# Batch 0 of a local-attention plus token-mixing MoE kernel as one hand-ordered pipeline

## The chip, the cores and the metric

The kernel runs on one core of a Trainium2 chip. The metric is the device time of one execution in microseconds, and the number to forecast is the median of several runs of the changed kernel. Engine names are those of the profile: PE is TensorE (matmuls), PEld its weight loads, DVE is VectorE, ACT is ScalarE, POOL is GpSimd, SP is SyncE, and SPq is the part of SP that issues DMAs.

## The reference, cut to what matters

Eight batches, eight heads, 576 tokens, head size 64. Heads 0 to 3 attend to the last 32 tokens (plain); heads 4 to 7 attend to 32 tokens at a distance of 4 (dilated). The attention output, 576 rows of 512, goes through a token-mixing low-rank product and a two-layer MLP.

```python
rel = pos[:, None] - pos[None, :]
mask_plain = (rel >= 0) & (rel < window)                     # window 32
mask_dil = (rel >= 0) & (rel < window * dilation) & (rel % dilation == 0)
scores = scale * np.matmul(q, k.transpose(0, 1, 3, 2))       # masked with -1e9
scores = scores - np.max(scores, axis=-1, keepdims=True)
attn = np.exp(scores)
attn = attn / (np.sum(attn, axis=-1, keepdims=True) + 1e-09)
x = np.matmul(attn, v)            # heads side by side: (8, 576, 512)
h = x.transpose(0, 2, 1) @ U @ V  # U 576x32, V 32x576
u = x + h.transpose(0, 2, 1)
out = u + np.maximum(u @ w_ch1, 0.0) @ w_ch2   # 512 -> 2048 -> 512
```

## The kernel before, in words

**Groups.** The tokens of a half (plain or dilated, the dilated ones sorted by residue so that its window is local too) are cut into nine tiles of 64 queries with 96 keys each. Two neighbouring tiles make a group of four units, so a batch has nine groups and the kernel 72. In batch 0 and 1 a unit is one tile and two heads: the queries of the two heads stand block-diagonally in a 128x128 operand, and one fp32 matmul (`s`, L380) gives 128 rows by 96 keys. From batch 2 on (`two`, L369) a unit is one head and 128 queries, and its operands are split into a high and a low fp32r part by ACT (L344) and POOL (L345, L348).

**Steps of a group.** `score` does the `s` matmuls. `soften` does mask and row minimum on DVE (L400, with L397 ahead of it from batch 2 on) and the exponential on ACT (L404), which also accumulates the row sums. `turn` transposes p: in batches 0 and 1 on PE (`ptp`, L417) with a DVE copy to SBUF (L421), later on DVE (L430, L433). `weighted` does four `pv` matmuls (L441), the reciprocal of the sums (L442, L443), and four DVE multiplications into `x` for plain tiles or `xp` for dilated ones (L469); the dilated rows then go to their place in `x` by small DMAs (L473).

**Token mixing.** When a batch is complete, `split` makes a high and a low part of x (ACT L487, DVE or POOL L489), `t_mm` multiplies by U (`t`, L509), `t_evict` copies the result in parts, `mix` multiplies by V (`m`, L533) and DVE adds to x (L535).

**MLP.** 12 chunks of 384 tokens. `transp` turns x (L564, later by DVE and DMA) and splits it into `uth`, `utl` (L569, L570). For each of 16 slices f of the hidden layer, `layer1` does 12 matmuls into `ph` (L733), ACT makes `hh` (L738), DVE `hl` (L739), and `layer2` adds nine matmuls to `acc` (L750). The attention and mixing of later batches are put between the matmuls by a table of due positions (`queue`, `slot`).

**Weights.** U, V, w1 and w2 come as float64 in pieces. `weight_step` moves four pieces on by one stage each: `fetch64` (DMA, SP, L194, L196), `narrow_a` (two ACT passes, L203, L204), `narrow_b` (DVE shift L208 and add L210) and the finish, for w1 and w2 `narrow_c` (cast on ACT L214 or DVE L216, remainder on POOL L217). Slice f needs pieces 3+2f and 4+2f.

**Order.** Before, the whole kernel is written in a program order from which a scheduler with priorities decides each engine's stream. Batch 0's operands are loaded by SP; all DMAs of the kernel are issued by SP. The program has eight DMA semaphores which it uses in rotation, so a DMA is issued only when the one eight places earlier has landed. Batch 0 stands wholly ahead of the first chunk; batch 1 is woven into chunk 0.

## Time and profile before

| what | value |
|---|---|
| runs (3) | 1029.8, 1030.41, 1031.37 us; median 1030.41 |
| the profiled execution | 1034.31 us, span of its instructions 1032.5 us, mean granted clock 0.974 |
| PE busy | 994.2 us, 96% of the span |
| PEld, DVE, ACT, POOL busy | 894.7, 645.1, 413.7, 289.5 us |
| chain that ended last | PE 82% |
| first `ph` matmul (start of chunk 0) | 66.39 us |
| first output add of chunk 0, 1, 2, 3 (L775) | 168.23, 263.85, 342.27, 421.12 us |

The profiled execution is 3.9 us above the median; its own time is 1.8 us above its span. A busy share is that of records: matmul ends are modelled, so a PE at 100% is not a PE at its peak. Rows of the timeline give start, duration, engine, line, operation, tiles and the count merged into the row; what stands in brackets at the end is the idle time before it and what ended it.

### The profile page before, as it was taken

How to read it: one execution, taken by the hardware profiler on the slowest of the kernel's cores; microseconds unless marked ns; L12 is line 12 of the kernel's file. 1: busy time of each engine (PE TensorE's matmuls, PEld its weight loads, DVE VectorE, ACT ScalarE, POOL GpSimd, SP SyncE). 2: the span in 40 equal slices, each digit the busy share in tenths (PEclk: the TensorE clock that was granted, in tenths of full speed). 3: DMA queues.
4: the chain of work that ended last, by engine and by line, in shares of the span. 5: the costliest groups of instructions: out<-in, count | busy, mean ns of one | idle time of the engine just before them, and what ended most of it. 6: DMA issues, size and time to landing. Idle time of an engine off the chain costs nothing.

```text
span 1032.5 us, 17337 instructions
## 1 busy us (share of the span) xinstructions
PE 994.2 (96%) x5328; PEld 894.7 (87%) x5328; DVE 645.1 (62%) x2188; ACT 413.7 (40%) x1233; POOL 289.5 (28%) x492
## 2 busy tenths in 40 slices
PE   6589998999999999999999999999999999999998
PEld 6468896998899898998899898999889898999997
DVE  4989768777457863877557873787637874311211
ACT  3867655444234532544333532445424442111110
POOL 0335433243132621434222531325213431000000
PEclk9669898999999999999999999999999999999999
DMA  9658544243232423434232432434223321400000
GB/s 262 206 186 259 182 139 119 76 114 102 64 102 77 123 81 76 120 85 116 74 90 81 124 89 61 129 84 126 85 72 88 115 66 30 126 1 1 31 1 31
DMA packets 96908, 103.03 MB, mean 100 GB/s; under 512 B 12817, under 2 KB 83537, under 8 KB 96817
## 3 DMA queue, kind: packets, MB, share of 16 engines
q1 hardware_dynamic: 96816, 101.94, 34.1%
q8 instruction: 43, 0.70, 0.3%
q14 instruction: 49, 0.39, 0.1%
HBM read 79.86 MB, written 17.30 MB: 94 GB/s over the span
## 4 chain that ended last, share of the span: by engine, by line
PE 82%; DVE 4%; DMA 1%; ACT 1%; issue 1%; POOL 0%; SPq 0%; DVEq 0%; ACTq 0%; POOLq 0%
PE ph L733 36%; PE acc L750 35%; PE pv L441 5%; PE s L369 3%; PE t L509 2%; DVE utl L570 1%; PE s L380 1%; PE m L533 1%; DVE pt L433 1%; DMA raw<-w 1%; DVE pt L430 0%; DMA qkr<-qk 0%; DVE x L469 0%; DVE v L210 0%; DMA x<-xp 0%
## 5 line engine op out<-in xcount | busy, mean ns | idle before, releaser
L750 PE MATMUL acc<-w2h,hh 128*128 128x512 f32 x576 | 228.8, 397 | 0.0
L750 PE MATMUL acc<-w2l,hh 128*128 128x512 f32 x576 | 228.3, 396 | 0.0
L750 PE MATMUL acc<-w2h,hl 128*128 128x512 f32 x576 | 214.0, 397 | 1.7 <-DVE hl L739 1.7
L345 POOL TENSOR_TENSOR qks<-qkr,qks 128x160 fp32r<-128x160 f32 x192 | 104.2, 542 | 379.8 <-ACT qks L344 273.1
L739 DVE SCALAR_TENSOR_TENSOR hl<-ph,hh 128x384 fp32r<-128x384 f32 x192 | 105.9, 552 | 165.2 <-ACT hh L738 164.9
L738 ACT ACTIVATE hh<-ph 128x384 fp32r<-128x384 f32 x192 | 93.3, 486 | 278.0 <-PE ph L733 268.0
L733 PE MATMUL ph<-uth,w1h 128*128 128x384 f32 x768 | 176.3, 343 | 0.1
L404 ACT ACTIVATE p<-p,nmax 128x160 f32<-128x160 f32 (+1 forms) x288 | 116.8, 406 | 148.8 <-DVE nmax L400 140.0
L733 PE MATMUL ph<-uth,w1l 128*128 128x384 f32 x768 | 174.4, 340 | 0.4 <-POOL w1l L217 0.4
L733 PE MATMUL ph<-utl,w1h 128*128 128x384 f32 x768 | 172.3, 338 | 0.0
L733 PEld LDWEIGHTS ph<-uth,w1h 128*128 128x128 f32 x768 | 139.7, 191 | 15.7 <-ACT uth L569 0.7
L733 PEld LDWEIGHTS ph<-uth,w1l 128*128 128x128 f32 x768 | 136.8, 190 | 1.2 <-POOL w1l L217 0.7
L733 PEld LDWEIGHTS ph<-utl,w1h 128*128 128x128 f32 x768 | 135.2, 188 | 1.4
L750 PEld LDWEIGHTS acc<-w2h,hl 128*128 128x128 f32 x576 | 107.7, 189 | 24.8 <-DVE hl L739 2.9
L430 DVE STREAM_TRANSPOSE pt<-p 32x128 f32<-32x128 f32 x384 | 115.9, 302 | 20.8 <-ACT p L404 15.6
L750 PEld LDWEIGHTS acc<-w2h,hh 128*128 128x128 f32 x576 | 108.6, 189 | 15.6
L750 PEld LDWEIGHTS acc<-w2l,hh 128*128 128x128 f32 x576 | 108.6, 189 | 15.0
L344 ACT CAST qks<-qkr 128x288 fp32r<-128x288 f32 x192 | 81.3, 428 | 86.6 <-PE s L369 58.4
L348 POOL TENSOR_TENSOR qks<-qkr,qks 64x128 fp32r<-64x128 f32 x192 | 89.9, 468 | 15.1
L397 DVE TENSOR_TENSOR p<-s,wide_sb 128x160 f32<-128x160 f32 x192 | 60.3, 319 | 48.6 <-PE s L369 46.6
L441 PE MATMUL pv<-v,pt 96*128 96x128 f32 x576 | 81.4, 287 | 7.2 <-DVE pt L421 7.2
L489 POOL TENSOR_TENSOR xhl<-x,xhl 128x256 fp32r<-128x256 f32 (+1 forms) x70 | 50.4, 739 | 130.4 <-ACT xhl L487 69.3
(66 smaller groups left out, 1023.2 us busy)
## 6 DMA issues: line engine op xcount, KB each, us to landing
qkr<-qk SPq DMA_DIRECT2D x192, 144.0 KB, 2.2
raw<-w SPq DMA_DIRECT2D x26, 512.0 KB, 4.6
v<-vv SPq DMA_DIRECT2D x126, 96.0 KB, 2.0
out<-x SPq DMA_DIRECT2D x36, 256.0 KB, 2.2
zd<-z SPq DMA_DIRECT2D x120, 64.0 KB, 2.1
xt<-zd SPq DMA_DIRECT2D x30, 256.0 KB, 2.8
qk<-qk SPq DMA_DIRECT2D x9, 448.0 KB, 9.2
qkr<-qk SPq DMA_DIRECT2D x18, 224.0 KB, 3.9
```

The source lines that it names most:

```text
L344: nc.scalar.copy(out=t[:, 0:QK2], in_=raw)
L345: nc.gpsimd.tensor_tensor(out=t[:, QK2:], in0=raw[:, P:], in1=t[:, P:QK2].bitcast(F32), op=ALU.subtract)
L348: eng.tensor_tensor(out=t[lo, 0:P], in0=raw[lo, 0:P], in1=t[lo, 0:P].bitcast(F32), op=ALU.subtract)
L397: nc.vector.tensor_tensor(out=p_sb[:, u, :], in0=sp[:, 0:KW], in1=wide_sb[:, kind], op=ALU.add)
L404: nc.scalar.activation(out=p_sb[:, u, 0:w], in_=p_sb[:, u, 0:w], func=AF.Exp, bias=nmax[:, u:u + 1], scale=-1.0, accum_out=ssum[:, u:u + 1],)
L430: nc.vector.transpose(out=to[:, :, WIN * (r % 2):WIN * (r % 2 + 1)], in_=p_sb[rs, :, QB * s + WIN * k:QB * s + WIN * (k + 1)])
L441: nc.tensor.matmul(pv[:, u, :], lhsT=pt[:, u, :], rhs=v_sb[:, u % 2, :], start=True, stop=True)
L489: eng.tensor_tensor(out=xl[rs], in0=x[rs], in1=xh[rs].bitcast(F32), op=ALU.subtract)
L733: nc.tensor.matmul(ph, lhsT=w[:, k, :], rhs=u[:, k, :], start=(n == 0), stop=(n == len(seq) - 1))
L738: nc.scalar.activation(out=hh, in_=ph, func=AF.Relu)
L739: nc.vector.scalar_tensor_tensor(out=hl, in0=ph, scalar=0.0, in1=hh.bitcast(F32), op0=ALU.max, op1=ALU.subtract)
L750: nc.tensor.matmul(acc[i], lhsT=h[:, ss], rhs=w, start=(f == 0 and n == 0), stop=(f == FC - 1 and n == 2))
```

## The change

1. **Order.** Batch 0 is written out by hand (`first_batch`), and inside `manual_schedule` the streams of PE, DVE, ACT and SP are exactly as written; POOL's is not. Per turn g: `s` of group g, `ptp` of g-1, `pv` of g-2, softmax of g, the copy of `pt` of g-1, `place` of g-3.
2. **Own DMA ring.** Batch 0's q, k, v and all weight pieces are issued by ACT instead of SP. All 36 loads of batch 0 and the first five pieces (ut, vt and three of w) stand ahead of ACT's first exponential, with ACT's table load behind them.
3. **Compact q.** The zeros of the block-diagonal q are not loaded: two memsets (POOL, DVE) clear `q_sb`, two DMAs per group fill the blocks.
4. **Rows by token, ones beside v, in every batch.** A unit is one head and both tiles of a group. `pv` is eight matmuls with 64 weight columns and 65 moving columns, the two tiles going to partitions 0 to 63 and 64 to 127; the 65th column of v is one, so it yields the row sum and ACT accumulates none. `place` does the reciprocal and one multiplication of 128x256 (two of 64x256 where the two tiles go to different places) instead of four of 64x128.
5. **In batch 0 alone:** the copy of `pt` moves from DVE to ACT; `t` is an fp32 matmul of unsplit x with fp32 U (`t_first`, ten of them), which drops the ten splits; the zero part of `ts` is a memset.
6. **Dilated tiles first** in each batch, and their half of the mixing first.
7. **Part of U and V first.** ut holds the blocks that batch 0 needs (10 instead of 14 columns of 32), vt the middle 384 columns of V; the rest (`uv`) follows behind the first slice of weights. The adds of these pieces and of the first two w pieces move from DVE to POOL.
8. **Weights.** Ahead of the third `uth` ACT's stream has both passes of `narrow_a` for two w pieces (slice 0) and one for two more; before, it had both for seven and one for an eighth. The order of issue inside chunk 0 is the scheduler's in both.

```diff
-TILES = [(0, j) for j in range(NJ)] + [(1, NJ - 1)] + [(1, j) for j in range(NJ - 1)]
+VW = D + 1
+TILES = [(1, j) for j in range(NJ)] + [(0, NJ - 1)] + [(0, j) for j in range(NJ - 1)]
...
-                nc.sync.dma_start(out=r, in_=src[:, h * step:(h + 1) * step])
+                nc.scalar.dma_start(out=r, in_=src[:, h * step:(h + 1) * step])
...
+    def load_q(g):
+        t = early.tile([P, UNITS, KB], F32, tag="k", name=f"k{g}", bufs=NGB)
+        nc.scalar.dma_start(out=t, in_=k0[g])
+        for i in range(2):
+            rs = slice(i * QB, (i + 1) * QB)
+            nc.scalar.dma_start(out=q_sb[rs, g, i], in_=q0[g, rs])
+        loaded[g, 0] = t
...
         nc.scalar.activation(
             out=p_sb[:, u, 0:w], in_=p_sb[:, u, 0:w], func=AF.Exp,
-            bias=nmax[:, u:u + 1], scale=-1.0, accum_out=ssum[:, u:u + 1],
+            bias=nmax[:, u:u + 1], scale=-1.0,
         )
...
+    def product(g, pt):
+        pv = psum.tile([P, UNITS, VW], F32, tag="ps", name=f"pv{g}")
+        for u in range(UNITS):
+            for i in range(2):
+                rs = slice(i * QB, (i + 1) * QB)
+                nc.tensor.matmul(pv[rs, u, :], lhsT=pt[:, u, rs], rhs=loaded[g, 1, i][:, u, :], start=True, stop=True)
+        return pv
...
+        if todo[0][1] is todo[1][1]:
+            todo = [(slice(0, P),) + todo[0][1:]]
+        for rs, x, row, half in todo:
+            n = rs.stop - rs.start
+            dst = x[row:row + n, 0:HALF_D]
+            nc.vector.tensor_tensor(
+                out=dst.rearrange("p (u d) -> p u d", u=UNITS), in0=pv[rs, :, 0:D],
+                in1=ssum[rs].unsqueeze(2).broadcast_to([n, UNITS, D]), op=ALU.mult)
...
+        nc.tensor.matmul(t_ps[0, c], lhsT=u32[rs, u * RANK:(u + 1) * RANK], rhs=x[rs],
+                         start=first, stop=t_count[c] == len(parts))
...
+        for g in range(NGB):
+            for u in range(UNITS):
+                score(g, u)
+            if g >= 1:
+                tp[g - 1] = turn_pe(g - 1, state.pop(g - 1)[0])
+            if g >= 2:
+                pv[g - 2] = product(g - 2, pt.pop(g - 2))
+            for u in range(UNITS):
+                soften(g, u)
+            if g >= 1:
+                copy(g - 1)
+            if g >= 3:
+                place(g - 3, pv.pop(g - 3))
...
+    order = tc.manual_schedule(engines=ORDERED)
+    order.__enter__()
     for g in range(NGB):
-        load_qk(g)
...
+        load_q(g)
         load_v(g, 0)
+        if g in U_AT:
+            pipe[U_AT.index(g)] = fetch64(U_AT.index(g))
+    send(NSMALL + 3)
+    first_batch()
+    order.__exit__(None, None, None)
```

Three places show what stands where. ACT's stream at its start, before (p is the probabilities, nmax the row minimum, ssum the row sum):

```order
L404 ACT_TABLE_LOAD
L404 ACTIVATE p_132,ssum_134<-p_132,nmax_133 128x96 x4
L404 ACTIVATE p_148,ssum_150<-p_148,nmax_149 128x96 x4
L404 ACTIVATE p_186,ssum_188<-p_186,nmax_187 128x96 x4
L404 ACTIVATE p_225,ssum_227<-p_225,nmax_226 128x96 x4
```

The exponentials of group 0 are the second thing ACT does. ACT's stream after, at the end of its issues (k, q, v are batch 0's operands, w the float64 weights):

```order
L305 DMA q_sb<-q 64x256 x2
L313 DMA v_158<-vv 96x520
L179 DMA raw_160<-w 128x4x256
L181 DMA raw_162<-w 128x1024
L179 DMA raw_164<-w 128x4x256
L417 ACT_TABLE_LOAD
L417 ACTIVATE p_166<-p_166,nmax_167 128x96 x4
L417 ACTIVATE p_181<-p_181,nmax_182 128x96 x4
L640 COPY pt_73<-ptp_188 96x512
```

The exponentials now stand behind 41 DMA issues and the table load. PE's stream in batch 0 before, from its first matmul:

```order
L380 MATMUL s_135<-qk_93 128x96 x4
L380 MATMUL s_151<-qk_99 128x96 x4
L417 MATMUL ptp_164<-id_sb,p_132 96x128 x4
L380 MATMUL s_189<-qk_103 128x96 x4
L417 MATMUL ptp_202<-id_sb,p_148 96x128 x3
L441 MATMUL pv_174<-v_97,pt_75 128x128 x4
L417 MATMUL ptp_202<-id_sb,p_148 96x128
```

And after, from its fifth group on:

```order
L451 MATMUL pv_287<-v_118,pt_73 64x65 x8
L394 MATMUL s_319<-k_132,q_sb 128x96 x4
L428 MATMUL ptp_324<-id_sb,p_275 96x128 x4
L451 MATMUL pv_329<-v_124,pt_74 64x65 x8
L394 MATMUL s_363<-k_140,q_sb 128x96 x4
L428 MATMUL ptp_368<-id_sb,p_317 96x128 x4
```

The order of the three steps is fixed, and `pv` is eight matmuls of half the width instead of four. ACT's stream before, from the third `uth` (the last that chunk 0's first matmul needs) to the first `hh`:

```order
L569 CAST uth_624<-tp_649 128x4x128
L204 ACTIVATE raw_619<-raw_619 128x512
L214 CAST w1h_82<-v_644 128x4x128
L203 ACTIVATE v_681<-raw_647 128x512
L204 ACTIVATE raw_647<-raw_647 128x512
L203 ACTIVATE v_690<-raw_669 128x512
L204 ACTIVATE raw_669<-raw_669 128x512
L214 CAST w2h_84<-v_666 128x512
L203 ACTIVATE v_699<-raw_684 128x512
L204 ACTIVATE raw_684<-raw_684 128x512
L738 ACTIVATE hh_0_785<-ph_0_752 128x384
```

After, seven instructions (the cast of w2h, an issue for w, three issues for batch 1's q and k, two casts of us) stand between the third `uth` and these, which end with the first `hh` (us and vs are the parts of U and V that later batches use, v_607 the rest of U and V, the other v and raw are w pieces):

```order
L188 ACTIVATE v_607<-raw_448 128x448
L189 ACTIVATE raw_448<-raw_448 128x448
L188 ACTIVATE v_631<-raw_164 128x512
L188 ACTIVATE v_636<-raw_450 128x512
L181 DMA raw_639<-w 128x1024
L188 ACTIVATE v_725<-raw_595 128x512
L189 ACTIVATE raw_595<-raw_595 128x512
L218 CAST us<-v_607 128x4x32
L212 CAST vs<-v_607 128x64
L212 CAST vs<-v_607 128x256
L179 DMA raw_728<-w 128x4x256
L826 ACTIVATE hh_0_688<-ph_0_656 128x384
```

Between the third `uth` and the first `hh` ACT had nine instructions and now has 18, six of them DMA issues.

More of the change, by code (lines that the diff above doesn't have):

```diff
@@ L59 @@
 H_ON_ACT = 3
-XL_DVE = ((0, 1), (1, 1))
+XL_DVE = ((1, 0),)
 AHEAD = 2
@@ L434, in turn @@
[L434 to L442 removed]
+                o = WIN * k + (QB * (r // 2) if is_wide(g) else 0)
+                nc.vector.transpose(out=pt[WIN * k:WIN * (k + 1), :, rs], in_=p_sb[rs, :, o:o + WIN])
@@ new lines, in turn, with weighted, place @@
+        return pt
+    def weighted(g, pt):
+        place(g, product(g, pt))
+    def product(g, pt):
[5 more added lines that the diff above has]
+        return pv
+    def place(g, pv):
+        b = g // NGB
+        ssum = work.tile([P, UNITS], F32, tag="ssum", name=f"ssum{g}", bufs=2)
+        nc.vector.tensor_scalar(out=ssum, in0=pv[:, :, D], scalar1=1e-9, scalar2=None, op0=ALU.add)
@@ L453, in weighted @@
             else:
-                if xp is None:
+                if i == 0:
                     if b == 0:
-                        xp = early.tile([P, HALF_D], F32, tag="xp", name=f"xp{g}", bufs=XPS)
-                    elif b < SPLIT and g % 2:
-                        xp = spare[:, 0:HALF_D]
-                    else:
-                        xp = work.tile([P, HALF_D], F32, tag="xp", name=f"xp{g}", bufs=1)
-                    part = next(p for p, js in enumerate(DPART) if j in js)
-                row = QB * DPART[part].index(j)
@@ L827, in lay_out @@
+    for a in range(4):
+        blocks[a] = U[a * P:(a + 1) * P]
+        blocks[4 + a] = U[64 + a * P:64 + (a + 1) * P]
+    blocks[8, 0:64] = U[512:576]
+    blocks[8, 64:128] = U[0:64]
+    perm = np.array([token_of(1, s) for s in range(S)])
+    ut = np.zeros((P, NU, RANK), raw)
+    for i, a in enumerate(UB):
+        ut[:, i] = blocks[a]
+    for p in range(NDP):
+        rows = perm[P * p:P * (p + 1)]
+        ut[:len(rows), len(UB) + p] = U[rows]
     vt = np.zeros((4, RANK, P + S), raw)
```

490 lines of the change are left out of this document (259 added, 231 removed).

## The prediction

> **What bounds the kernel now.** I read three views: the busy time by stretch, to see where PE is the bound; then the timeline of the start, because the change is there; then the groups of the first chunk. First the stretches (columns: length, then PE, PEld, DVE, ACT, POOL busy, granted clock, DMA share, GB/s).
>
> ```profile
> 0.00:10.00 10.00, 3.75 (x16) 3.51 (x17) 1.15 (x10) 2.82 (x9) 1.20 (x6) 1.00 0.79 236
> 10.00:20.00 10.00, 7.90 (x56) 7.39 (x56) 7.09 (x45) 4.63 (x24) 0.00 (x0) 0.95 1.05 272
> 20.00:30.00 10.00, 9.00 (x69) 8.52 (x68) 7.56 (x37) 5.47 (x23) 0.00 (x0) 0.88 1.04 319
> ...
> 0.00:66.40 66.40, 42.92 (x221) 35.40 (x221) 48.32 (x179) 36.42 (x120) 13.44 (x17) 0.75 0.73 215
> 66.40:120.90 54.50, 50.40 (x275) 46.46 (x275) 52.06 (x137) 43.11 (x111) 29.66 (x23) 0.90 0.71 227
> 120.90:168.20 47.30, 46.78 (x269) 40.57 (x268) 32.73 (x93) 25.64 (x77) 13.34 (x15) 1.00 0.45 132
> 168.20:178.70 10.50, 6.82 (x25) 4.55 (x24) 9.52 (x27) 4.90 (x16) 3.92 (x8) 0.71 0.53 155
> 178.70:263.90 85.20, 85.15 (x465) 78.11 (x466) 64.31 (x250) 37.73 (x120) 31.15 (x61) 0.98 0.35 97
> 342.30:421.10 78.80, 78.80 (x428) 71.14 (x427) 49.19 (x164) 30.11 (x90) 24.27 (x46) 1.00 0.34 94
> ```
>
> From 178.7 us on PE has no gap, so only fewer or shorter matmuls help there. The change can win in four places: the 66.4 us ahead of chunk 0; its first half, 66.4 to 120.9, where DVE (52.06 of 54.50 us) is the fullest engine; its second half, which PE bounds; and the border of chunks 0 and 1, 168.2 to 178.7. The profiled execution took 1034.31 us against a median of 1030.41; I apply the differences to the median.
>
> **The change part by part.**
>
> *Loads ahead of the first exponential.* Now ACT exponentiates at 6.46 us; after, its stream holds 41 DMA issues first. Timeline rows are start, length, engine, line, operation, tiles, count, and in brackets the idle time ahead and what ended it; SPq issues DMAs.
>
> ```profile
> 0.74 1.28 ACT L404 ACT_TABLE_LOAD   x1 [0.74 <-PEq L847]
> 2.59 0.43 SPq L295 DMA_DIRECT2D qk<-qk  x1
> 6.46 0.37 ACT L404 ACTIVATE p<-p,nmax 128x96 f32<-128x96 f32 x1 [4.44 <-DVE nmax L400]
> 6.74 0.19 ACT L404 ACTIVATION_READ_ACCUMULATOR p<-p,nmax 128x1 f32 x1
> 28.42 0.39 SPq L194 DMA_DIRECT2D raw<-w  x1
> ```
>
> An issue waits for the DMA eight places earlier, so ACT's last one waits until about 4.93 MB (in units of 1000 KB of 1024 bytes; 5.05 million bytes) have landed: eight groups of 515 KB, ut, vt and half a piece of w. The first two rows of stretches moved 2.36 + 2.72 = 5.08 MB in 20 us. Hence 20 us, 0.4 us for the last issue (the 0.39 and 0.43 us rows) and 1.28 us for the table: first exponential at 21.7 us, 15.2 later. Here a rule bears. The Trainium skill, "DMA: Bandwidth & Descriptors", section "Issuing engines are not separate DMA queues", says that DMAs started by different engines share the same 16 DMA engines, and that a second issuer saves only issue time. The share of 1.05 and 1.04 agrees; were it wrong and a second ring brought the 319 GB/s of the third row from the start, 5.05 MB would take 15.8 us and the sum below would be 4.2 us less. The memsets of q and the compact q (4.6 instead of 5.8 MB for q, k and v) lie inside these 20 us, and SP, which issues these loads today, only gets emptier.
>
> *The nine groups.* With operands there, PE sets the pace:
>
> ```profile
> 11.25 0.69 DVE L421 COPY pt<-ptp 96x512 f32<-96x512 f32 x1
> 13.82 1.20 DVE L469 TENSOR_TENSOR x<-pv,ssum 64x128 f32<-64x128 f32 x4 [0.42 <-PE pv L441]
> ...
> 24.99 0.60 PE L417 MATMUL ptp<-id_sb,p 128*96 128x128 f32 x4
> 25.42 1.06 PE L441 MATMUL pv<-v,pt 96*128 96x128 f32 x8
> 26.32 0.28 PE L417 MATMUL ptp<-id_sb,p 128*96 128x128 f32 x1
> 26.43 1.03 PE L380 MATMUL s<-qk 128*128 128x96 f32 x8
> 27.30 0.38 PE L417 MATMUL ptp<-id_sb,p 128*96 128x128 f32 x2
> ...
> 58.36 0.42 DVE L535 TENSOR_TENSOR x<-x,m 128x256 f32<-128x256 f32 x1 [0.78 <-PE m L533]
> ```
>
> From start to start, ptp takes 0.43, pv 0.90, s 0.87 us: 2.2 us a group. ACT needs four exponentials of 0.28 (6.74 less 6.46; the read of the sum falls away) and the copy of 0.69 that it takes from DVE, 1.8; DVE needs less. Eight groups of 2.2 are 17.6 us, the last four exponentials 1.1, the first fp32 `t` 4 x 0.44 = 1.8 (0.44 is twice an s matmul of 0.22; bounds 0.2 and 0.9), a cold stretch of PE 1 to 2: last exponential at about 44 us. The cost of the eight `pv` is put at today's (the last part of this list gives its bounds). `place` with 128x256 lies between the 0.42 us of one add of that size and the 1.20 of four multiplications; I take 0.8.
>
> *The tail to the first `ph`* (timeline).
>
> ```profile
> 57.63 0.47 PE L509 MATMUL t<-xhl,us_d 128*64 128x256 f32 x1 [1.30 <-DVE xhl L489]
> 65.76 0.58 ACT L569 CAST uth<-tp 128x512 fp32r<-128x512 f32 x1
> 66.39 1.65 PE L733 MATMUL ph<-uth,w1h 128*128 128x384 f32 x4
> 66.81 0.62 ACT L214 CAST w1h<-v 128x512 fp32r<-128x512 f32 x1
> 67.31 0.69 ACT L203 ACTIVATE v<-raw 128x512 f32<-128x512 f32 x1
> 68.46 0.67 ACT L203 ACTIVATE v<-raw 128x512 f32<-128x512 f32 x1
> ```
>
> Today's last `t` to the first `ph` is 8.8 us (57.63 to 66.39). Ahead of it come the last group's ptp 0.43, copy 0.69, pv 0.90, place 0.8: 2.8 us. First `ph` at 44 + 11.6, about 55.6 us: **−10.8**. Without the splits it could be 2 earlier; with `t` at 0.9 us, 3 later.
>
> *Chunk 0, first half.* What ACT had narrowed early it narrows now under chunk 0.
>
> ```profile
> 72.17 0.49 ACT L738 ACTIVATE hh<-ph 128x384 fp32r<-128x384 f32 x1 [0.81 <-PE ph L733]
> 120.93 0.49 ACT L738 ACTIVATE hh<-ph 128x384 fp32r<-128x384 f32 x1 [0.29 <-PE ph L733]
> ```
>
> And of the groups of the first 150 us one of POOL (line, engine, tiles, count; busy, mean ns):
>
> ```profile
> L217 POOL TENSOR_TENSOR w1l<-v,w1h 128x512 fp32r<-128x512 f32 x14 | 20.0, 1432 | 29.8 <-ACT w1h L214 15.1 <-DVE w1h L216 11.3 <-DVE ssum L442 3.0
> ```
>
> From the third `uth` to the ninth `hh` ACT's stream holds, before, 19 + 18 passes of `narrow_a`, 15 casts, 24 exponentials and nine `hh`; it took 55.2 us (65.76 to 120.93). After, it holds 48 passes (0.57 each from start to start, 67.31 to 68.46): 27.4 us; 18 casts of 0.50 (66.81 to 67.31): 9.0; 25 issues of 0.4: 10.0; 16 exponentials of 0.28: 4.5; nine `hh` at 0.4 (0.49 less the overlap of the next): 3.6; five small casts of 0.3: 1.5. That is 56 us, and ACT becomes the bound in DVE's place. With 2 to 4 us in which it waits for `ph` or a DMA, 59: **+3.8** (+0.8 with no wait, −3 if PE set the pace at 52). So the ninth `hh` stands at about 114, 7 earlier. POOL takes over the adds of five pieces at up to 1.43 us an instruction; its 29.66 busy of 54.50 us leave room.
>
> *What is left over.* By the ninth `hh` batch 1 is two groups behind today (16 exponentials for 24). Those 4.4 us of PE fall into the second half, where PE has no slack: **+4** (3.5 to 4.4).
>
> *The border.* Today the last rows of batch 1 reach x by a DMA, as the chain of waits shows there (start, length, what):
>
> ```profile
> 162.71 0.58 SPq L473
> 163.34 1.86 DMA x<-spare
> ```
>
> The split of x waits for its landing. The first output add of chunk 0 follows, and it is the start of the border:
>
> ```profile
> 168.23 1.89 DVE L775 TENSOR_TENSOR x<-acc,x 128x512 f32<-128x512 f32 x3 [0.84 <-PE acc L750]
> ```
>
> With dilated tiles first, the plain ones end the batch and no DMA lies ahead of the last mixing. The 10.5 us at the border hold 6.82 of PE at a clock of 0.71, which is 4.8 at full clock: at most 5.7 us can go. I take **−4** (0 to −5.7), since transposes and splits stay.
>
> *`pv` in 63 later groups.* First two groups of weight loads (270 to 660 us), then the timeline around one `pv`:
>
> ```profile
> L441 PEld LDWEIGHTS pv<-v,pt 96*128 96x128 f32 x216 | 27.8, 191 | 0.7
> L509 PEld LDWEIGHTS t<-xhl,us 128*64 128x64 f32 x48 | 6.1, 134 | 1.4 <-issue 0.4
> ```
>
> ```profile
> 324.44 1.05 PE L441 MATMUL pv<-v,pt 96*128 96x128 f32 x8
> 325.25 0.48 PE L750 MATMUL acc<-w2l,hh 128*128 128x512 f32 x1
> ```
>
> Eight records take 0.81 to 0.90 us from start to start, about 110 ns each, of a weight load of 191; so 80 of the 191 ns overlap the next. A load of 64 columns has 134, less 80 is 54 to 57: sixteen such make 0.91 instead of 0.89, 63 times **+1.3**. If loads kept their ratio (134 to 191), 16 x 77 ns is 1.24 and the sum gains +22; if the two halves of the array ran side by side it is −28 (first rival). I take the difference because both rows are of the same unit. The `L750` row starts where the next step follows. The missing sums on ACT and shorter `place` on DVE in later batches cost or win nothing while PE has no gap.
>
> Sum: −10.8 + 3.8 + 4 − 4 + 1.3 = −5.7, from 1030.4 to about **1025**.
>
> **The rivals.** *B, the halves overlap.* Two tiles of 64 columns on different halves could load and multiply at once: pv 0.46 us, −0.45 x 63 = −28, giving about 997. The pv rows speak against it: pace there goes with the load of weights, and one loader is seen busy at a time. The Trainium skill, "TensorEngine Tiling (Array Packing)", section "Key Properties", says that different tiles can execute loads and matmuls in parallel; no row of this trace shows two tiles at work. *C, ACT does not bound chunk 0* (its waits fall into what PE leaves): +3.8 becomes −3 to −6, and the time 1012 to 1018. For it: DVE loses a quarter of its work there. Against: the 56 us. *D, swallowed:* the start is won but the narrowing that moved under chunk 0 gives all of it back, within 0.2% of 1030, about what a measurement of this kernel can tell from no change. For it: the pieces are as many as before, and every one left out ahead is done later. *E, the other side:* ACT's queue blocks. In the first half 25 of its instructions are issues, each standing until a DMA eight places back has landed, with `hh` behind it, for which PE waits.
>
> ```profile
> raw<-w SPq DMA_DIRECT2D x26, 512.0 KB, 4.6
> qk<-qk SPq DMA_DIRECT2D x9, 448.0 KB, 9.2
> ```
>
> The columns are the count, the size of one and the median time from issue to landing. Pieces of 512 KB take 4.6 us to land and under a full queue 448 KB took 9.2. If each of 25 issues stands 0.55 us longer, that is +14, about 1039; it decides from some 8 us of such waits. Against it: the share of 0.71 in that stretch leaves the queue free a quarter of the time.
>
> **How the numbers follow.** The main case, 1019 to 1030, has 0.47, of which 0.05 within 0.2% of today; B 0.12; C 0.13; D 0.13; E 0.15. Faster: 0.42 + 0.12 + 0.13 = 0.67; same: 0.05 + 0.13 = 0.18; slower 0.15. The range takes in the main case, C, D and the nearer half of E: 1006 to 1036 leaves out B and the far half of E.
>
> **What would show it.** The first exponential at 20 to 23 us, pv's 16 records near 0.9 us a group, the first `ph` at 54 to 58, the ninth `hh` at 112 to 117, ACT over 90% busy between these, PE without a gap in the second half, and a border under 7 us. A pv of 0.5 us shows B; an ACT with under 80% busy and the ninth `hh` before 109 shows C; ACT idle ahead of its issues in chunk 0 shows E. The forecast is wrong above all if the price of a 64-column weight load is not the difference I took, or if the weights of the first slices come too late behind ACT's queue.

## The result, and the profile after

The changed kernel takes 1046.33 us (median of four runs, 1046.05 to 1047.01) against 1030.89 for the kernel before: a ratio of 1.0147, 95% interval 1.0128 to 1.0167. It is slower by 15.4 us where 5 to 6 us faster was forecast. The profiled execution took 1047.01 us, 0.7 above its median; the one shown of the kernel before stood 3.9 above its own.

The time by stretch, first as in the prediction and then in three parts: up to the first `ph`, on to chunk 1's first `hh`, the rest (length; PE, PEld, DVE, ACT, POOL busy; granted clock; DMA share; GB/s). Of the kernel after:

```profile
0.00:10.00 10.00, 3.79 (x15) 3.58 (x16) 2.78 (x9) 0.00 (x0) 3.78 (x9) 1.00 0.74 191
10.00:20.00 10.00, 0.55 (x3) 0.30 (x2) 0.80 (x8) 0.00 (x0) 0.00 (x0) 1.00 1.04 253
20.00:30.00 10.00, 3.22 (x14) 2.88 (x15) 0.03 (x1) 3.98 (x10) 0.00 (x0) 1.00 1.02 290
30.00:40.00 10.00, 10.00 (x81) 8.75 (x80) 3.72 (x30) 5.49 (x16) 0.00 (x0) 1.00 0.07 17
...
68.80:125.40 56.60, 46.81 (x262) 40.25 (x263) 52.50 (x105) 46.21 (x95) 36.58 (x29) 0.93 0.83 268
125.40:188.40 63.00, 55.53 (x363) 45.12 (x363) 39.82 (x123) 28.60 (x79) 18.49 (x21) 0.95 0.42 120
188.40:196.50 8.10, 4.72 (x21) 3.47 (x20) 7.52 (x24) 4.76 (x11) 4.31 (x9) 0.76 0.74 224
...
0.00:68.80 68.80, 40.03 (x290) 31.85 (x290) 21.98 (x116) 24.74 (x65) 10.50 (x15) 0.96 0.49 130
68.80:201.10 132.30, 111.66 (x662) 93.44 (x663) 102.41 (x260) 80.75 (x187) 60.82 (x60) 0.92 0.62 191
201.10:1045.10 844.00, 839.20 (x4954) 742.38 (x4953) 468.90 (x1596) 282.09 (x695) 227.31 (x426) 1.00 0.29 80
```

And of the kernel before, the row from 30 to 40 us and the same three parts:

```profile
30.00:40.00 10.00, 6.03 (x26) 4.35 (x27) 9.71 (x40) 9.82 (x38) 1.42 (x2) 0.63 0.72 200
...
0.00:66.40 66.40, 42.92 (x221) 35.40 (x221) 48.32 (x179) 36.42 (x120) 13.44 (x17) 0.75 0.73 215
66.40:184.40 118.00, 109.65 (x589) 97.22 (x589) 97.93 (x272) 75.34 (x210) 48.88 (x49) 0.91 0.58 178
184.40:1032.50 848.10, 841.61 (x4522) 762.03 (x4520) 498.87 (x1738) 301.94 (x905) 227.14 (x426) 1.00 0.28 80
```

The start is not shorter but 2.4 us longer. The middle is 14.3 us longer. The rest is 4.1 shorter. In the first two parts together PE, DVE and ACT have no more work than before: PE 151.7 us against 152.6, DVE 124.4 against 146.3, ACT 105.5 against 111.8. Only POOL, which took over adds, has more, 71.3 against 62.3, and PE hardly waits for it (0.5 us in the middle, 0.4 before). What grew is idle time. In the first part DVE is busy for 22 of 68.8 us where it was for 48 of 66.4. Of these 26 us, 10.6 are its shifts and adds of weights (1.6 us instead of 12.2); the others the change dropped, merged or gave to ACT. From 30 to 40 us the transfers run at 17 GB/s where the kernel before brought weights at 200, and by the first `ph` seven transfers of weights have landed instead of eleven. The conversion left over comes later: DVE's shifts and adds take 53.5 us in the middle instead of 43.3.

The start of the kernel after in the timeline:

```profile
25.05 1.28 ACT L417 ACT_TABLE_LOAD   x1 [25.05 <-DMA q_sb<-q]
26.35 2.23 ACT L417 ACTIVATE p<-p,nmax 128x96 f32<-128x96 f32 x8
33.66 1.06 PE L428 MATMUL ptp<-id_sb,p 128*96 128x128 f32 x4
34.65 1.14 PE L451 MATMUL pv<-v,pt 96*64 96x65 f32 x16
35.71 2.11 PE L394 MATMUL s<-k,q_sb 128*128 128x96 f32 x8
37.65 0.60 PE L428 MATMUL ptp<-id_sb,p 128*96 128x128 f32 x4
38.18 0.69 PE L451 MATMUL pv<-v,pt 96*64 96x65 f32 x16
38.80 2.11 PE L394 MATMUL s<-k,q_sb 128*128 128x96 f32 x8
40.74 0.60 PE L428 MATMUL ptp<-id_sb,p 128*96 128x128 f32 x4
```

The first exponential comes at 26.35 us. From start to start `ptp` takes 0.53 and `pv` 0.62 us, but `s` 1.94 (38.80 to 40.74), where it took 0.87: a group is 3.09 us, not 2.2. Ahead of 37.6 us `ptp` and `pv` run at half that pace (0.99 and 1.06 us), and `s` at the same 1.94. The view's clock column reads 1.00 for both, so this slow pace of a PE that has just begun is not in it.

The tail, with DVE's and ACT's rows:

```profile
62.51 0.58 ACT L589 CAST uth<-tp 128x512 fp32r<-128x512 f32 x1 [1.65 <-PE tp L584]
63.12 0.69 DVE L590 TENSOR_TENSOR utl<-tp,uth 128x512 fp32r<-128x512 f32 x1 [1.37 <-ACT uth L589]
63.73 0.41 DVE L555 TENSOR_TENSOR x<-x,m 128x256 f32<-128x256 f32 x1
64.20 1.11 PE L584 MATMUL tp<-id_sb,x 128*128 128x128 f32 x4 [1.61 <-DVE x L555]
65.35 0.58 ACT L589 CAST uth<-tp 128x512 fp32r<-128x512 f32 x1 [2.26 <-PE tp L584]
68.83 1.65 PE L821 MATMUL ph<-uth,w1h 128*128 128x384 f32 x4 [0.68 <-ACT uth L589]
```

This is a ring: DVE's add of the next tile (L555) stands behind the `utl` of this one, which waits for `uth`, which waits for the transposes, which wait for the add. Three rounds, 2.84 us from one `uth` to the next.

What PE waited for between the first `ph` and chunk 1's first `hh` (total, times, longest; the first rows), after and then before:

```profile
PE acc L838 <- ACT hh L826: 8.8, 6, 2.9
PE tp L584 <- DVE nmax L413: 2.5, 1, 2.5
```

```profile
PE pv L441 <- DVE pt L421: 4.1, 2, 2.8
PE m L533 <- DVE x L535: 2.5, 2, 1.6
```

PE's idle time in this part is 20.6 us (132.30 less 111.66) against 8.4, and 8.8 of the 12.3 more is a wait for `hh`, which does not occur before; 6.3 of it lie ahead of the ninth `hh`. What stands ahead of one such `hh` in ACT's rows:

```profile
74.47 0.47 ACT L826 ACTIVATE hh<-ph 128x384 fp32r<-128x384 f32 x1
...
81.69 0.68 ACT L189 ACTIVATE raw<-raw 128x512 int32<-128x512 uint32 x1 [0.59 <-DMA raw<-w]
83.38 0.62 ACT L199 CAST w1h<-v 128x512 fp32r<-128x512 f32 x1 [0.46 <-DVE v L195]
86.06 0.62 ACT L199 CAST w2h<-v 128x512 fp32r<-128x512 f32 x1 [0.93 <-DVE v L195]
86.59 0.48 ACT L826 ACTIVATE hh<-ph 128x384 fp32r<-128x384 f32 x1
```

Between the first `hh` and the second lie 12.1 us of passes over weights. ACT is idle for 2.8 of them, for transfers and for DVE; the others are its own work, with five issues among it.

### The profile page after: what moved, and what is told of

Its sections match the earlier page's. It is cut to its first block, busy times and chain, and to the rows that moved or that the text cites. A ratio compares the mean times of both kernels' runs of the same rounds, so it can differ in the third digit from the quotient of the medians.

```text
span 1045.1 us, 17970 instructions
## 1 busy us (share of the span) xinstructions
PE 990.9 (95%) x5904; PEld 867.7 (83%) x5904; DVE 593.3 (57%) x1972; ACT 387.6 (37%) x946; POOL 298.6 (29%) x501
## 4 chain that ended last, share of the span: by engine, by line
PE 83%; DVE 3%; DMA 2%; issue 1%; ACT 1%; SPq 0%; ACTq 0%; DVEq 0%
PE acc L838 37%; PE ph L821 36%; PE pv L451 4%; PE s L381 3%; PE t L531 2%; PE m L553 1%; DMA raw<-w 1%; PE s L394 1%; DMA zd<-z 1%; DMA v<-vv 0%; DVE v L195 0%; DVE x L555 0%; DVE z L563 0%; PE ptp L428 0%; ACT v L188 0%
## 5 line engine op out<-in xcount | busy, mean ns | idle before, releaser
L838 PE MATMUL acc<-w2h,hl 128*128 128x512 f32 x576 | 211.3, 399 | 1.1 <-DVE hl L827 1.1
L821 PE MATMUL ph<-utl,w1h 128*128 128x384 f32 x768 | 175.6, 341 | 0.0
L821 PE MATMUL ph<-uth,w1h 128*128 128x384 f32 x768 | 172.7, 343 | 1.6 <-DVE w1h L201 0.7
L821 PE MATMUL ph<-uth,w1l 128*128 128x384 f32 x768 | 171.8, 340 | 0.5 <-POOL w1l L202 0.5
L417 ACT ACTIVATE p<-p,nmax 128x160 f32<-128x160 f32 (+1 forms) x288 | 109.6, 406 | 132.5 <-DVE nmax L413 131.4
L440 DVE STREAM_TRANSPOSE pt<-p 32x128 f32<-32x128 f32 x432 | 130.1, 301 | 18.7 <-ACT p L417 13.3
L838 PEld LDWEIGHTS acc<-w2h,hh 128*128 128x128 f32 x576 | 108.6, 189 | 26.8 <-ACT hh L826 10.6
L500 POOL TENSOR_TENSOR xhl<-x,xhl 128x256 fp32r<-128x256 f32 (+1 forms) x65 | 47.3, 736 | 98.3 <-ACT xhl L498 94.4
L413 DVE CUSTOM_DVE_ANT_0 p<-s,p 128x160 f32<-128x160 f32 x192 | 60.0, 321 | 4.1
```

Source lines behind the costliest of these rows:

```text
L413: nc.vector.tensor_tensor_reduce(out=p_sb[rs, u, 0:w], in0=a, in1=c, scale=-1.0 / 8.0, scalar=3.0e38, op0=ALU.add, op1=ALU.min, accum_out= ...
L417: nc.scalar.activation(out=p_sb[:, u, 0:w], in_=p_sb[:, u, 0:w], func=AF.Exp, bias=nmax[:, u:u + 1], scale=-1.0,)
L440: nc.vector.transpose(out=pt[WIN * k:WIN * (k + 1), :, rs], in_=p_sb[rs, :, o:o + WIN])
L500: eng.tensor_tensor(out=xl[rs], in0=x[rs], in1=xh[rs].bitcast(F32), op=ALU.subtract)
L821: nc.tensor.matmul(ph, lhsT=w[:, k, :], rhs=u[:, k, :], start=(n == 0), stop=(n == len(seq) - 1))
L838: nc.tensor.matmul(acc[i], lhsT=h[:, ss], rhs=w, start=(f == 0 and n == 0), stop=(f == FC - 1 and n == 2))
```

## The experiments

All times are device times; intervals are 95%. "Middle" is from the first `ph` to chunk 1's first `hh`, "rest" from there to the end. These two and the first `ph` are those of the profiled execution, the time is the median.

| kernel | median us | ratio to before | first ph | middle | rest |
|---|---|---|---|---|---|
| before | 1030.89 | | 66.4 | 118.0 | 848.1 |
| after | 1046.33 | 1.0147 (1.0128 to 1.0167) | 68.8 | 132.3 | 844.0 |
| q_same_dma | 1046.69 | 1.0147 (1.0124 to 1.0170) | 66.2 | 134.1 | 843.6 |
| w_on_sp | 1047.76 | 1.0164 (1.0133 to 1.0195) | 69.8 | 131.3 | 843.6 |
| mixes_first | 1036.31 | 1.0056 (1.0033 to 1.0079) | 68.4 | 127.2 | 843.6 |
| pv_by_half | 1061.69 | 1.0290 (1.0245 to 1.0334) | 76.8 | 128.5 | 857.4 |
| weights_15_steps | 1050.90 | 1.0177 (1.0145 to 1.0210) | 72.4 | 133.3 | 843.9 |
| plain_first_later | 1050.49 | 1.0189 (1.0148 to 1.0229) | 67.4 | 131.8 | 847.9 |
| start_mended | 1039.16 | 1.0071 (1.0047 to 1.0096) | 63.5 | 127.4 | 843.6 |
| loads_on_sp | 1037.70 | 1.0058 (1.0035 to 1.0080) | 54.7 | 136.7 | 844.2 |
| unordered | 1040.44 | 1.0089 (1.0074 to 1.0104) | 76.0 | 118.7 | 843.6 |
| start_w4 | 1042.23 | 1.0101 (1.0084 to 1.0118) | 69.4 | 130.6 | 843.6 |
| sp_start | 1031.29 | 0.9990 (0.9978 to 1.0002) | 50.3 | 135.5 | 843.6 |
| sp_unordered | 1022.73 | 0.9917 (0.9899 to 0.9935) | 47.1 | 128.5 | 843.6 |
| after_asked_early | 1047.26 | 1.0146 (1.0111 to 1.0180) | 73.1 | 130.1 | 843.6 |
| before_asked_early | 1036.05 | 1.0046 (1.0030 to 1.0062) | 67.7 | 120.2 | 848.0 |
| sp_unordered_early8 | 1018.74 | 0.9869 (0.9845 to 0.9893) | 46.9 | 125.4 | 844.1 |
| sp_unordered_early12 | 1021.80 | 0.9891 (0.9862 to 0.9921) | 47.6 | 124.5 | 843.6 |
| ten_less | 1044.76 | 1.0135 (1.0107 to 1.0163) | 73.4 | 129.4 | 843.6 |
| ten_less_before | 1026.87 | 0.9969 (0.9956 to 0.9983) | 66.7 | 113.6 | 848.0 |

The first `ph` of mixes_first, weights_15_steps, after_asked_early, ten_less and start_w4 is about 4 to 6 us late for one reason: in those executions PE kept its slow pace through most of batch 0 (a group took some 4 us). So it did in pv_by_half, whose `pv` are longer besides. It seems to vary from run to run: of mixes_first's six runs four took 1035.4 to 1036.3 us and two 1041.0 and 1041.2, the profiled one among the latter. Only a profiled execution shows the pace, so that it is what parts the two groups of times is likely and not shown.

**q_same_dma.** The weight load of q reads neighbouring columns.

```diff
-                ql, kr = q_sb[:, g].rearrange("p i (q u) -> p u (i q)", u=UNITS)[:, u], loaded[g, 0][:, u]
+                ql, kr = q_sb[:, g].rearrange("p i x -> p (i x)")[:, P * u:P * (u + 1)], loaded[g, 0][:, u]
```

> The changed kernel, but each weight load of q in batch 0 reads 128 columns that lie side by side instead of every fourth one (the columns are then the wrong queries; the transfers stay as they are). Theory: the distance of 16 bytes between columns is what makes an s record 233 ns against 110 in the kernel before; 72 records give back 8.9 us, the first ph comes at about 60 instead of 68.8 us, and 5 to 9 us of it reach the end (1037 to 1041 us). Rival: the slow s is PE's cold start or the order written by hand; then s stays at 233 ns and the time at 1046.

Its PE rows:

```profile
33.76 1.13 PE L394 MATMUL s<-k,q_sb 128*128 128x96 f32 x8
34.73 0.60 PE L428 MATMUL ptp<-id_sb,p 128*96 128x128 f32 x4
35.26 0.69 PE L451 MATMUL pv<-v,pt 96*64 96x65 f32 x16
35.88 1.13 PE L394 MATMUL s<-k,q_sb 128*128 128x96 f32 x8
```

`s` takes 0.97 us and a group 2.12. So the distance of 16 bytes between columns cost 1 us a group, which the prediction had put at nothing. The last exponential comes 5.5 us earlier (47.7), the first `ph` 2.6, and the end does not move at all. The tail behind the last exponential took 18.5 us instead of 15.7: with the groups done earlier ACT waits 1.1 us in it for a weight piece, and PE is at its slow pace again (a row of four `t` takes 1.92 us, in the changed kernel 1.05).

**mixes_first.**

```diff
 for i in range(CT):
     mix(0, i, 0)
+for i in range(CT):
     transp(i)
```

> The changed kernel, with the three last mixes of batch 0 ahead of the three transposes instead of one by one. Theory: between the last t and the first ph the three rounds of 2.84 us are a ring, in which DVE's add of the next tile stands behind the utl of this one; without it the first ph comes 3 to 4 us earlier than 68.8 and the end 2 to 4 us earlier. Rival: PE or ACT set the pace of these rounds, or the weights do behind them; then the first ph moves by under 1 us or the end does not follow.

```profile
66.81 1.07 ACT L589 CAST uth<-tp 128x512 fp32r<-128x512 f32 x2 [1.65 <-PE tp L584]
67.77 0.60 ACT L589 CAST uth<-tp 128x512 fp32r<-128x512 f32 x1
```

The ring is gone: the three `uth` stand 0.5 us apart instead of 2.84. From the last cast of `ts` (ACT, L544) to the first `ph` it is 3.6 us instead of 8.3, and 4.8 in start_mended below, which has the same order. From the last exponential it is 10.2 us (58.2 to 68.4) instead of 15.7, but that figure belongs to a batch 0 at the slow pace, in which the weights had come in time; in start_mended it is 14.8. The middle, too, is 5 us shorter, with 4.6 us of waits for `hh` instead of 8.8, which was not expected and whose cause is not shown. The time fell by 10 us, where 2 to 4 were expected.

**w_on_sp.** Theory: the DMA issues in ACT's queue block it.

```diff
-nc.scalar.dma_start(out=r, in_=src[...])
+(nc.scalar if i < NSMALL + 3 else nc.sync).dma_start(out=r, in_=src[...])
```

> The changed kernel, with the weight pieces behind the first three issued by SP again. Theory (ACT's queue blocks): in the second half of chunk 0 the pieces of the last three slices stand in ACT's stream behind splits of x that wait for small transfers; on SP they are issued near 120 to 150 us instead of 149 to 176, the first output add of chunk 0 comes 8 to 15 us earlier than 188.4, and the whole kernel takes 1031 to 1038 us. Rival: the pieces wait for buffers that x and its splits hold because the dilated half now comes first; then they stay near 150 to 176 us and the time within 2 us of 1046.

The theory falls. The pieces of the last three slices are issued from 144 us instead of 149, and the time is the same (1047.76). PE's waits for `hh` are down to 0.7 us, but others stand in their place (the first rows):

```profile
PE acc L838 <- DVE hl L827: 3.7, 4, 1.6
PE tp L584 <- DVE x L555: 2.2, 1, 2.2
PE ph L821 <- ACT w1h L199: 2.0, 2, 1.8
```

**pv_by_half.**

```diff
-for u in range(UNITS):
-    for i in range(2):
+for i in range(2):
+    for u in range(UNITS):
         rs = slice(i * QB, (i + 1) * QB)
         nc.tensor.matmul(pv[rs, u, :], ...)
```

> The changed kernel, with the eight pv matmuls of a group in another order: first the four of one half of the array, then the four of the other, in place of turns. Theory: in the changed kernel the two halves work at once (pairs of records start 6 ns apart, 55 ns from pair to pair); in this order they can't, a pv goes from 0.62 to 0.9 us or more, and over 63 groups the time rises by about 18 us. Rival: the pace is that of loading 64 columns and the pairs are only how records are written; then pv stays at 0.62 us and the time at 1046.

A `pv` in the steady part, with the records around it, in this kernel, in the changed one and in the one before:

```profile
486.79 0.86 PE L821 MATMUL ph<-utl,w1h 128*128 128x384 f32 x4
487.58 0.97 PE L451 MATMUL pv<-v,pt 96*64 96x65 f32 x16
488.48 0.41 PE L381 MATMUL s<-qks 128*128 128x320 f32 x1
```

```profile
487.08 0.69 PE L821 MATMUL ph<-utl,w1h 128*128 128x384 f32 x3
487.70 0.69 PE L451 MATMUL pv<-v,pt 96*64 96x65 f32 x16
488.31 0.45 PE L821 MATMUL ph<-utl,w1h 128*128 128x384 f32 x1
```

```profile
492.79 0.86 PE L733 MATMUL ph<-uth,w1l 128*128 128x384 f32 x4
493.49 1.05 PE L441 MATMUL pv<-v,pt 96*128 96x128 f32 x8
494.30 0.37 PE L533 MATMUL m<-ts,vs 128*128 128x256 f32 x1
```

The eight matmuls take 0.90 us half by half and 0.61 in turns; the four of before took 0.81. The two halves of the array do work at once, and by half the kernel is 15.4 us slower (rest 857.4 instead of 844.0), where about 18 were expected. But the record just ahead of a `pv` is longer in both new kernels: over some 42 `pv` between 300 and 900 us, an `acc` record ahead lasts 327 ns from start to start (median) instead of 233, a `ph` record 268 instead of 174. The record just behind is longer, too, though less: over the whole rest 338 instead of 317 for `acc`, 282 instead of 260 for `ph`. So 0.194 us is won and 0.116 given back each time, about 4.2 us over the 54 groups of the rest, and the rest is 4.1 shorter (844.0 against 848.1). That the two agree does not settle it: plain_first_later, below, has the same `pv` and the same longer records, and its rest is as long as before. The Trainium skill, "TensorEngine Tiling (Array Packing)", section "Key Properties", says both: tiles run independently, and a change of the tiling mode drains the array. This trace agrees with the two: pairs of records start 6 ns apart, and the record ahead of the change is 94 ns longer.

**weights_15_steps, plain_first_later.** Two theories for the long second half of chunk 0: the splits of batch 1 hold the buffers that the last slices' pieces need, or dilated tiles first make those splits wait.

```diff
-PRE_N = 5
+PRE_N = 15
```

> The changed kernel, with 15 instead of five steps of the weights written ahead of chunk 0. No instruction is added or dropped; only the order changes in which the last three slices' pieces and the splits of batch 1's x ask the one pool for buffers. Theory (buffers): in the changed kernel five splits hold their buffers when the pieces of slices 13 to 15 ask, in the kernel before two; with 15 steps four halves are issued before the splits again, the last three hh come about 8 us earlier, the first output add at 176 to 182 us instead of 188.4, the whole kernel takes 1034 to 1041 us. Rival (the second half is long because ACT and the transfers are late by the whole first half, or because dilated tiles come first): the add stays within 3 us of 188 and the time at 1044 to 1047.

```diff
+TILES1 = [(0, j) for j in range(NJ)] + [(1, NJ - 1)] + [(1, j) for j in range(NJ - 1)]
...
-        return TILES[2 * (g % NGB) + i]
+        return (TILES if g < NGB else TILES1)[2 * (g % NGB) + i]
...
```

> The changed kernel, with plain tiles first again from batch 1 on (batch 0 as changed). Theory (dilated first costs the second half): the splits of batch 1's first half no longer wait 8 us for small transfers of dilated rows, the first output add comes 5 to 10 us earlier than 188.4, the border to chunk 1 gets 3 to 4 us longer again, the time is 1040 to 1044 us. Rival (buffers alone): the pieces still ask behind five splits, the add stays within 3 us of 188, the border gets longer, 1046 to 1050 us.

Both fall. With 15 steps the first pieces go out at 145.5 us, four together as expected, and the middle stays at 133. With plain tiles first the middle is 131.8 and the rest grows to 847.9, so dilated tiles first are worth some 4 us in the later batches of this kernel and are not what chunk 0 lost by. The border, from the first output add to chunk 1's first `ph`, stays at 7.1 us, where both expectations had it longer.

**start_mended, loads_on_sp, sp_start.** start_mended lays q out by unit, so that its columns stand side by side, and has mixes_first's order. loads_on_sp gives the loads back to SP. sp_start does both.

```diff
-nc.scalar.dma_start(out=q_sb[rs, g, i], in_=q0[g, rs])
+nc.scalar.dma_start(out=q_sb[rs, g, :, i], in_=q0[g, rs].rearrange("p (u q) -> p u q", u=UNITS))
...
```

> The changed kernel with q's 128 weight columns of a unit side by side (the transfers of q write runs of 256 bytes) and the three mixes ahead of the three transposes. Theory (the start is not what the time hangs on): the first ph comes at 60 to 63 us instead of 68.8, but the weights behind it give most of it back, and the first output add comes only 3 to 6 us earlier; 1036 to 1042 us. Rival (the start counts in full): 6 to 9 us at both places, 1037 us or less, and 1030 if the two add up with what the mixes alone gave.

```diff
-nc.scalar.dma_start(
+nc.sync.dma_start(
```

> The changed kernel with all the loads that ACT issues (q, k, v, weights) issued by SP, in the same order. Theory (ACT's first exponential waits for its own 41 issues): it comes at 4 to 7 us instead of 26.4, the groups follow the transfers, which need some 25 us for all nine, so the last exponential comes at 42 to 46 instead of 53 us and the first ph 6 to 10 us earlier; the end follows by 0 to 5 us. Rival (the transfers set the start, whoever issues them): the last exponential stays within 3 us of 53.

> start_mended, with all its loads issued by SP. Theory A (the starts add up): first ph at 46 to 50 us, and the gain of loads_on_sp and of start_mended together, 1029 to 1033 us. Theory B (what is won ahead of chunk 0 is mostly lost in it, since the weights' conversion on DVE and ACT takes its time after the first ph): chunk 0 takes 120 us or more and the time is 1034 to 1038 us.

With the loads on SP the first exponential comes at 8.4 us, the last at 34.1 and the first `ph` at 54.7, 14 us earlier, the last two further than expected, but the middle is 4.4 us longer and 8.6 reach the end. The two starts add up (1031.29, no difference from before that can be measured): first `ph` at 50.3, with a middle of 135.5. start_mended by itself has the first `ph` 5.3 us earlier and the end 7.2, within the range expected of the first theory; its first output add comes 9.8 us earlier, which neither had. So each start counts, though behind loads_on_sp's a part is given back. In start_mended it is the order of the mixes that counts: mixes_first, without the new layout of q, took 1036.31, and q_same_dma won nothing, so no run shows the layout to be worth anything at the end.

**unordered, sp_unordered.** The same instructions without the order written by hand; sp_unordered is sp_start with that.

```diff
-    order = tc.manual_schedule(engines=ORDERED)
-    order.__enter__()
...
-    order.__exit__(None, None, None)
```

> The changed kernel without the order written by hand: the same instructions of batch 0, but a scheduler sets every engine's stream, as in the kernel before. Theory (the strict order keeps the conversion of weights out of batch 0): DVE then adds 14 pieces ahead of chunk 0's first hl, as the kernel before does (13), instead of 3; chunk 0, from its first ph to its first output add, takes 102 to 109 us instead of 119.6, whatever the start does; the time is 1032 to 1041 us. Rival (chunk 0 is long for a reason of its own: dilated tiles first, or the late issue of the last three slices): it takes over 115 us here too, and the time is 1042 us or more.

> sp_start without the order written by hand (the scheduler fills the gaps with conversion of weights). Theory (conversion in the gaps of batch 0 is what the hand order lost): chunk 0 takes 102 to 112 us and the time is 1020 to 1031 us, at or below the kernel before. Rival (the scheduler mixes up batch 0 and gives its gain back): first ph after 60 us and 1032 us or more.

The stretches of unordered:

```profile
0.00:75.90 75.90, 47.49 (x292) 34.99 (x292) 47.04 (x148) 46.66 (x108) 29.20 (x32) 0.83 0.76 235
75.90:181.90 106.00, 99.61 (x622) 85.17 (x623) 68.38 (x195) 53.10 (x130) 36.08 (x32) 0.95 0.44 131
181.90:194.70 12.80, 9.42 (x40) 8.18 (x39) 10.09 (x34) 5.95 (x14) 5.76 (x12) 0.73 0.70 194
```

Ahead of the first `ph` DVE is busy for 47 us instead of 22 and the transfers bring 235 GB/s instead of 130; the `ph` comes 7 us later, but the middle is 118.7 instead of 132.3, as in the kernel before, and PE's idle time in it 9.8. DVE's shifts and adds of weights take 27.7 us ahead of the first `ph` instead of 1.6, and 29.3 in the middle instead of 53.5. Chunk 1's first `hh` comes at 194.7 instead of 201.1, so start and middle together are 6.4 us shorter. The order by hand cost 6 us here (1046.33 to 1040.44) and 8.6 in the other pair (sp_start 1031.29, sp_unordered 1022.73). In sp_unordered the conversion did not move ahead of the first `ph` as expected, yet the middle is 7 us shorter than in sp_start.

**start_w4.** Two more pieces of weights converted inside the order by hand of start_mended.

```diff
...
+            if g == 3:
+                narrowed(w0)
+                add_low(w0, nc.vector)
+            if g == 4:
+                finish(w0)
+                narrowed(w1)
+                add_low(w1, nc.vector)
...
```

> start_mended, with four weight pieces converted inside the order written by hand instead of two, in gaps of DVE and ACT. Theory (each piece left to chunk 0 costs its 1.8 us of DVE there, where DVE is 93% busy): chunk 0 from first ph to first output add takes 3 to 6 us less than the 115.1 of start_mended, the start gets 0 to 2 us later, the time is 1034 to 1038 us against 1039. Rival (DVE is not what chunk 0 waits for): no change, 1037 to 1041 us.

The expectation failed: 1042.23, slower than start_mended. Its profiled execution had the slow pace in batch 0 (3.9 us a group), so its first `ph` of 69.4 says little, but the middle is longer too (130.6 for 127.4). Two pieces more at the start don't help by themselves.

**after_asked_early, before_asked_early, and the two on top of sp_unordered.** The pieces ask for buffers earlier: the edit of after_asked_early and early8. In early12 W_RATE is 12, and in the kernel before W_RATE alone goes to 8.

```diff
-PRE_N = 5
-W_RATE = 4
+PRE_N = 15
+W_RATE = 8
```

> The changed kernel, with the steps of the weights written so early (15 ahead of chunk 0, eight instead of four per slice) that the last three slices' pieces ask for the pool's buffers before all five splits of batch 1 (in the changed kernel behind all five). No instruction is added or dropped. Theory (buffers are given in the order of asking, and the pieces stood behind splits that come only with batch 1's first half): the first of these pieces is issued by 125 us instead of 149, all are by 160 instead of 176, the first output add comes 8 us or more earlier than 188.4; 1034 to 1040 us. Rival (DVE alone, which has 12 us more of weights to convert between the first ph and batch 1's first t): the issues move, the add stays within 4 us of 188, 1043 to 1050 us.

> The kernel before with eight steps of the weights per slice instead of four, so that its last pieces ask first, too. Theory (buffers): little to win here, since four of the halves were issued at 119 us already; 1024 to 1031 us. Rival (DVE alone): 1030 to 1034 us.

> sp_unordered (all loads on SP, q's columns side by side, mixes ahead of transposes, no order by hand) with 15 steps of the weights ahead of chunk 0 and eight per slice. Theory (buffers): the last slices are issued 10 us or more earlier, chunk 0 from first ph to first output add takes 102 to 110 us instead of 114, 1012 to 1020 us. Rival (DVE alone): 1020 to 1025 us.

> As sp_unordered_early8 with twelve steps per slice, so that the pieces ask earlier still. Theory (buffers): as there or 1 to 3 us better. Rival (DVE alone): conversion then crowds out batch 1's softmax on DVE, and the time is above that of sp_unordered, 1023 to 1030 us.

In after_asked_early all pieces are out by 145 us instead of 176, and chunk 0 ends 10.8 us sooner behind its first `ph` (108.8 instead of 119.6), but the way from the output add to chunk 1's first `hh` grows from 12.7 to 21.3 us; the time stays. So here the buffers set where the waiting stands, not how long it is. The kernel before gets slower by it, by 4 to 5 us, which neither theory had. On top of sp_unordered eight steps give 4 us: 1018.74, the best version, 1.3% below the kernel before; with twelve it is 1021.80, between the two expectations.

**ten_less, ten_less_before.** DVE's shift and add are left out for ten pieces; shown is the edit of the changed kernel (third to twelfth piece of w), in the kernel before it is the 13th to the 22nd.

```diff
 def add_low(i, eng):
-    narrow_b(*pipe[i], eng)
+    if not NSMALL + 2 <= i < NSMALL + 12:
+        narrow_b(*pipe[i], eng)
```

> The changed kernel without DVE's shift and add for ten pieces of w (the third to the twelfth), so that these weights have wrong values; transfers, ACT's passes, casts and POOL's remainders stay. It takes 10 x 1.75 = 17.5 us of DVE out of chunk 0. Theory (chunk 0 waits for DVE, which has 9 us more of weights to convert there than in the kernel before): from the first ph to chunk 1's first hh it takes 120 to 126 us instead of 132.3, and the time is 1034 to 1041 us. Rival (chunk 0 waits for ACT, for transfers or for the order of steps): under 3 us change, 1043 to 1048 us.

> The kernel before without DVE's shift and add for ten pieces of w (the 13th to the 22nd, which it converts in chunk 0), so that these weights have wrong values. Theory (DVE is near the bound in the first half here, too, but PE in the second): from the first ph to chunk 1's first hh 112 to 117 us instead of 118, 1024 to 1029 us. Rival (PE alone bounds chunk 0 here): no change, 1029 to 1033 us.

DVE's busy time in the middle fell by some 15 us in both, the middle by 2.9 us in the changed kernel and 4.4 in the control, the time by 1.6 and 4.0. So DVE's conversion alone is not what the changed kernel's chunk 0 waits for; my second theory of it falls, too.

## Why the prediction was wrong, step by step

| step | forecast | measured |
|---|---|---|
| first exponential | 21.7 us | 26.35 |
| a group | 2.2 us | 3.09 (4.0 at PE's slow pace) |
| last exponential to first ph | 11.6 us | 15.7 |
| first ph | 55.6 us | 68.8 |
| third uth to ninth hh | 59 us | 57.2 |
| ninth hh to first output add | 51.3 us | 63.0 |
| border, first output add to chunk 1's first ph | 6.5 us | 7.1 |
| pv and the rest | +1.3 us | −4.1 |

*Loads ahead of the first exponential.* The wait was right in kind and 4.7 us too small. By the rows above 4.44 MB had moved by 20 us and 5.9 by 25, where 5.05 were to do. The count took in only what was issued up to group 7's q; the transfers behind them run beside them and take their share. And the first 10 us moved 191 GB/s, not 236. That ACT's ring brings no more bandwidth held: shares of 1.04 and 1.02, as with SP. The choice of ACT as the issuer is what cost: with the same loads on SP the first exponential comes at 8.4 us and the end 8.6 earlier.

*The nine groups.* Wrong: the cost of the new operand layout was put at nothing. The diff shows the rearrangement with a distance between columns, and no row of the trace of before had such a load; the step should have carried a bound. It cost 1.0 us a group; `pv` gave 0.28 back, and `ptp` took 0.10 more. The cold stretch of 1 to 2 us came to some 2 (two groups at 4.0 us instead of 3.1).

*The tail.* Wrong: DVE's strict order makes a ring of three rounds, which the order of the instructions had shown. Without it the way from the last cast of `ts` to the first `ph` is 3.6 and 4.8 us instead of 8.3. The ring alone does not make the tail what was forecast: in start_mended it still takes 14.8 us, 1.2 of them ACT's wait for a weight piece.

*Chunk 0, first half.* Right in size (57.2 for 59), but that ACT's queue is the bound is not borne out: without most of its issues the stretch takes 61.8 us (w_on_sp), and with 15 us of DVE's work out of it 53.4 (ten_less). DVE is busy for 52.5 of the 56.6 us behind the first `ph`. What sets the pace there stays open, so the hit in size is partly luck. And PE fell behind further than counted: it did 46.8 us of work up to the ninth `hh` where it had done 50.4.

*Chunk 0, second half.* This step failed most: 63.0 us for 51.3. The forecast was 47.3 us full of PE's work and 4 left over from the first half. PE had 55.5 us of work there, 8.7 more than before instead of 4, and it stood idle for 7.5 us where no gap was forecast. The ground of rival E was found in part: PE waits for `hh` behind ACT's queue, 6.3 us in the first half and 2.5 in the second. But its mechanism, the issues, is not the cause: on SP they cost the same. Shown is that the middle goes from 132.3 to 118.7 us when the hand order goes, with a start 7 us longer, and that no single blocker (issues, tile order, buffers, ten pieces of DVE's work) takes more than 3 us away; the order of the last mixes takes 5. My reading is that the weights which the kernel before brings and converts in the gaps of batch 0 have to be brought and converted in chunk 0, where they share the in-order queues of ACT and DVE with `hh`, `hl` and batch 1, and each blocker that is removed uncovers the next. That reading is argued from these rows, not shown; open is also why sp_unordered's middle is shorter although its DVE converts no more ahead.

*The rest and the border.* The border came in size and not for its reason. It was to be short because plain tiles end the batch, but plain_first_later, where dilated tiles end it, has 7.1 us as well, and after_asked_early, with plain tiles last, 16.4. What sets it is not shown, and the hit is luck. `pv` was forecast at +1.3 with a rival of −28: the halves do overlap, as in rival B, but 16 loads of 64 columns don't halve the time, and what the change of mode costs ahead and behind takes over half of the gain. What part of the 4.1 us is `pv`'s and what part the tile order's stays open: the records add up to 4.2 for `pv`, and the tile order is worth 3.9 with `pv` as it is.

The start is 13.2 us later than forecast (4.7 the loads, 4.5 the groups, 4.1 the tail, each rounded), the second half 11.7 longer, the first half 1.8 shorter, the border 0.6 longer, the rest 5.4 better: +18.3. The other 3 us are the two executions' distances from their medians.

Which parts of the change cost the time is shown by undoing them one at a time: the loads on ACT 8.6 us (loads_on_sp), the mixes and transposes in turns 10.0 (mixes_first), the order by hand 5.9 (unordered). That is 24.5, and with all three undone and q laid out anew it is 23.6 (sp_unordered, 1022.73). The forecast had no term for the mixes, priced the loads only as a later start, and the order by hand only as ACT's narrowing under chunk 0 (+3.8) and what it leaves over (+4). That 1022.7 lies near its 1025 is chance, since the terms are others.

D's thought (each piece left out ahead is done later) had the right direction, but it took no account of a loss that could exceed the gain. In rival C the lower figure does not follow from its terms: −3 to −6 in place of +3.8 gives 1015 to 1018, not 1012.
